# A gated attention and mlp block on one core: value products split by columns, the first attention turn beside the mlp's last tile, mlp in text order, statistics fetched apart

## The chip, the cores and the metric

The kernel runs on one core of a Trainium2 chip. The metric is the device time of one execution in microseconds (us). The core's engines are named as in the profile: PE is TensorE (matmul), PEld its weight load, DVE VectorE, ACT ScalarE, POOL GpSimd, SP SyncE, which here only issues DMAs. Each engine works through its own queue of instructions in order and waits on semaphores for the others.

## What is computed

The input is x of 2048 tokens by 448. Cut to what matters, the reference is:

```python
g = sigmoid((x * gate_w).sum(-1, keepdims=True))
# attention: 16 heads of 28 channels
q, k, v = split(x @ wqkv)
p = softmax(q @ k.T * 28 ** -0.5)
a = (p @ v) @ wo
# mlp: 448 -> 1792 -> 448
b = gelu(layernorm(x) @ w1 + b1) @ w2 + b2
return g * a + (1 - g) * b
```

Inputs and output are fp32. For most matmuls the kernel splits each fp32 factor into a high and a low part in float32r, and adds three products (high by high, high by low, low by high).

## The kernel before, in words

TensorE's order is written by hand over the whole kernel. For the other engines a scheduler sets the order from dependences in the first two stages, and the text's order holds in the attention (`manual_schedule` at L664). The PSUM accumulator is one tile of eight banks of 512 fp32 columns.

Stage 1, the projections (L219 to L260). For each of four chunks of 512 tokens, `qk_tile` makes 7 tiles of q and k (11 matmuls of 512 columns, L168) that go through ACT and DVE to DRAM, and `v_tile` makes 4 tiles of v. Between them lie the layernorm statistics: `ln_stats` loads two token tiles and runs bn_stats and bn_aggr on DVE (L196 to L199), `ln_rows` makes the columns of mean and 1/deviation, and `ln_turn` (L207 to L214) turns them into rows: for each of the two a transpose on PE, a copy on DVE, a DMA to `lns`. `ln_turn` runs twice, for 4 and for 12 token tiles, and both of its loop's steps use one bank. `ln_load` reads the rows back, spread over all partitions; `ln_apply` normalises a tile of x on POOL and ACT.

Stage 2, the mlp (L472 to L498). For each chunk of 512 tokens, `mlp1(f)` makes 14 tiles of the hidden layer (11 matmuls each into bank f % 2), with the gelu twice on ACT (L454, L455) and the low part `hl` on POOL (L456). `mlp2(c, i)` then makes four output tiles of 42 matmuls (L463, L464, L466), copied on ACT to `h` (L469) and stored to `gbs` (L470). In chunk 0 the weights are loaded as they are needed: `load_w1` splits on ACT and POOL (L93, L94), `load_w2` on ACT and DVE (L99, L100). All share a staging buffer `r` of three (L85).

Between the mlp's matmuls lies other work for PE. A softmax needs the largest score of each query first; the class `RowMax` makes those maxima with single score products (L321) of 512 keys, reduced on DVE, one bank (L301) or two (L303) at a time. The class `Filler` hands them out: in the mlp in groups of six products into banks 2 to 7, spread evenly over its slots (476 of 1040 of them there), and in the attention up to three per turn, evenly (`due`).

Stage 3, the attention (L664 to L715). A unit is one score tile of 128 keys by 512 queries of one head; four units, one per head of a group of four, make a step. A turn does five units: three, then two, each with three products (L629), in banks 0 to 4, and an exp over three banks and one over two (L634), with up to three row maxima in banks 5, 6, 5. The third uses the bank of the first, and so waits for DVE's reduce of the first. Behind the scores, `pv_mm` (L655) adds the value products of the steps whose exps an earlier turn has made: four matmuls in fp32, one per head, in four column groups of 32 of the array, 512 columns each, into bank 7 (L658). 205 turns do 256 steps, so 153 turns add one step and 51 turns two. When 16 steps have been summed, `finish` normalises the result, in parts spread over later turns (`STEPS`); in the last group it goes on to the output projection.

At the seam between the mlp and the attention, the gate's exp and reciprocal (L611 to L614) come first; on SP's queue come the last store to `gbs` (L470), a load of b2 (L679), and the four loads of wo (`load_wo`, L590), each of which DVE casts to `woh` (L593) between the reduces of turns 1 to 4.

Of the kernel before, what the change touches and what calls it, by code (L numbers as in the profile page):

```python
# [7 lines left out]
F32 = mybir.dt.float32  # L8
# [7 lines left out]
P = 128  # L16
# [18 lines left out]
LQ = 12  # L35
STEPS = (2, 5, 7, 8, 9, 10)
# [3 lines left out]
def kernel(ctx: ExitStack, tc: tile.TileContext, xt, wqk, wv, wo, xk, w1, b1, w2, b2,  # L40
# [43 lines left out]
    def staged(width):  # L84
        return my.tile([P, CH], F32, name="r", bufs=3)[:, :width]  # L85

    def load_w1(f):
        r = staged(CH)
        nc.sync.dma_start(r, w1[f].rearrange("p t x -> p (t x)"))
        t = mw1.tile([P, 8, P], F32R, name=f"w1f{f}")  # L90
        w1h[f], w1l[f] = t[:, 0:4], t[:, 4:8]
        r = r.rearrange("p (t x) -> p t x", t=4)
# [3 lines left out]
    def load_w2(f):  # L96
        r = staged(D)
        nc.sync.dma_start(r, w2[f])
        nc.scalar.activation(w2h[f], r, AF.Copy)  # L99
        nc.vector.tensor_sub(w2l[f], r, w2h[f].bitcast(F32))  # L100
# [9 lines left out]
    def ln_fetch(c, t):  # L110
        lnx[c, t] = staged(CH)
        nc.sync.dma_start(lnx[c, t], xt[t, :, c * CH:(c + 1) * CH])
# [12 lines left out]
    with tc.tile_pool(name="qx", bufs=2) as qx, tc.tile_pool(name="qo", bufs=3) as qo, \  # L125
# [67 lines left out]

        def ln_stats(i):
            x = qx.tile([P, 2, D], F32, name="bxr")
            nc.sync.dma_start(x, xk[2 * i:2 * i + 2].rearrange("t p d -> p t d"))  # L196
            for n in range(2):
                nc.vector.bn_stats(st[:, 2 * i + n], x[:, n])
                nc.vector.bn_aggr(mv[:, 2 * i + n], st[:, 2 * i + n])  # L199
# [7 lines left out]
        def ln_turn(a, b):  # L207

            ps = next_ps()
            for n in range(2):  # L210
                r = qw.tile([b - a, P], F32, name=f"rows{a}{n}")
                nc.tensor.transpose(ps[:b - a, n * P:(n + 1) * P], mr[:, n, a:b], ident)
                nc.vector.tensor_copy(r, ps[:b - a, n * P:(n + 1) * P])
                nc.sync.dma_start(lns[n * NT + a:n * NT + b], r)  # L214
# [4 lines left out]
        for c in range(NC):  # L219
            for m in range(NM):  # L220
# [16 lines left out]
                if c == 0 and m in (3, 5):  # L237
                    ln_stats(m // 4)
                if c == 1 and m == 1:
                    ln_rows(0, TPC)  # L240
                if c == 1 and m == 5:
                    ln_turn(0, TPC)
                if c == 1 and m == 6:
                    ln_load(0)
                if c == 1 and m >= 4 or c == 2 and m < 3:
                    ln_stats(m - 2 if c == 1 else m + 5)
                if c == 2 and m in (0, 1, 2, 4):
                    ln_fetch(0, (0, 1, 2, 2, 3)[m])
                if c == 2 and 3 <= m < 6 or c == 3 and m == 0:
                    ln_apply(0, m - 3 if c == 2 else 3)  # L250
# [4 lines left out]
                if c == 3 and m < 3:  # L255
                    load_w1(m)
# [88 lines left out]
    class Filler:  # L345
# [11 lines left out]
        def spread(self, queue, upto, slots):  # L357
            if self.max is None:
                self.max = RowMax()
# [70 lines left out]


# [26 lines left out]
    def mlp2(c, i):  # L458

        sl = slice(i * P, (i + 1) * P)  # L460
        a = bank[:, i % 2, :D]
        for f in range(NF):
            nc.tensor.matmul(a, hh[f][:, sl], w2h[f], start=(f == 0), stop=False)  # L463
            nc.tensor.matmul(a, hh[f][:, sl], w2l[f], start=False, stop=False)  # L464
            filler.run(2)
            nc.tensor.matmul(a, hl[f][:, sl], w2h[f], start=False, stop=(f == NF - 1))  # L466
            filler.run(1)
# [4 lines left out]
    for c in range(NC):  # L472
        for f in range(NF):
            if c == 0 and f + 3 < NF:
                load_w1(f + 3)
            if c == 0 and f == 0:
                for k in range(4):
                    load_khr(0, k)
            if c == 0 and f == FS:
                filler.spread(nc.sync, MLP_MAX, (NC * NF - FS) * 23)  # L480
            if c == 0:
                load_w2(f)
            mlp1(f)
        if c == NC - 1:
            m0.close()
            aq = ctx.enter_context(tc.tile_pool(name="aq", bufs=1, side="right", reuse_waits="tile"))
            load_khi(0)
            load_klo(0)
            load_q(0)
            load_v(0)  # L490
            load_qm(0)
        else:
            ln_load(c + 1)
        for i in range(TPC):
            if c + 1 < NC:
                ln_fetch(c + 1, i)
                ln_apply(c + 1, i)
            mlp2(c, i)  # L498
# [7 lines left out]
    U, UA = 5, 3  # L506
# [103 lines left out]

    tc.keep_in_program_order(nc.scalar.activation(gate, zall, AF.Exp, scale=-1.0))  # L611
    nc.vector.tensor_scalar_add(gate, gate, 1.0)
    nc.vector.reciprocal(gate, gate)
    nc.vector.tensor_scalar(ngate, gate, -1.0, 1.0, op0=OP.mult, op1=OP.add)  # L614

    filler.spread(nc.gpsimd, NG * NC * 65, ((NG * NC - 2) * NT + LQ - 1) * 4 // U)

    probs = {}

    def scores(units, most):  # L620

        def product(u, i):
            n, k, j = u // 4 // NT, u // 4 % NT, u % 4
            g, (qh, ql) = n // NC, qs[n]
            a, b, r = ((khi[g], qh, DH + 1), (klo[g], qh, DH), (khi[g], ql, DH))[i]
            r = slice(32 * j, 32 * j + r)
            nc.tensor.matmul(bank[:, u % U], a[r, k * P:(k + 1) * P], b[r], start=(i == 0), stop=(i == 2))  # L629

        def exps(units):
            t = ap.tile([P, len(units), CH], F32, name=f"pt{len(units)}")
            b = units[0] % U
            nc.scalar.activation(t, bank[:, b:b + len(units)], AF.Exp, scale=SCALE)  # L634
            for i, u in enumerate(units):
                probs[u] = t[:, i]

        first, last = units[:UA], units[UA:]
        if most > 0:
            filler.max.issue(5, 1, [(first[0] + 3) % 4])  # L640
        for i in range(3):
            for u in first:
                product(u, i)
        exps(first)
        for i in range(3):
            for u in last:
                product(u, i)
            if i == 0 and most > 1:
                filler.max.issue(6, 1, [(first[0] + 1) % 4, (first[0] + 2) % 4])
        if last:  # L650
            exps(last)
        if most > 2:
            filler.max.issue(5, 1, [(first[0] + 1) % 4, (first[0] + 2) % 4])

    def pv_mm(step):  # L655
        n, k = divmod(step, NT)
        for j in range(4):
            nc.tensor.matmul(pv[32 * j:32 * j + 32, :], vg[n // NC][:, k, 32 * j:32 * j + 32], probs.pop(4 * step + j),  # L658
                             start=(k == 0), stop=(k == NT - 1), skip_group_check=True)

    pv = bank[:, 7]
    E = mybir.EngineType
    steps = NG * NC * NT
    with tc.manual_schedule(engines={E.SP, E.Pool, E.Activation, E.DVE}):  # L664
        fin = None
        summed = 0
        ready = 0
        at = -1
        since = 0
        for u in range(0, 4 * steps, U):  # L670
# [27 lines left out]
            scores(units, min(3, filler.due()))  # L698
            ended = False
            while summed < ready and not ended:  # L700
                pv_mm(summed)
                summed += 1
                ended = summed % NT == 0
            ready = (units[-1] + 1) // 4
            since += 1
            if ended:
                n = summed // NT - 1
# [4 lines left out]
        while summed < steps:  # L712
            pv_mm(summed)
            summed += 1
# [54 lines left out]
```

## Time and profile before

| | us |
|---|---|
| median of three runs | 1151.25 |
| lowest and highest of them | 1142.76, 1155.83 |
| the profiled execution | 1146.98 |
| its span, first to last instruction | 1145.2 |
| stage 1, from the first matmul | 6.7 to 126.7 |
| mlp | 126.7 to 486.4 |
| attention and tail | 486.4 to 1145.2 |

The mean granted clock of TensorE was 0.991. Lines of the page and of answers on the trace name a group of instructions by line of the kernel, engine, operation, and the tiles written and read, with partitions x elements and a count (x8). In the timeline the first number is the start in us, the second the duration, and a bracket at the end gives the idle time of the engine just before, with what ended it. In the windows view each row is a stretch of the span, with the busy time and instructions of each engine, the granted clock (PEclk, 1.00 is full), the share of the DMA engines and GB/s.

### The profile page before, as it was taken

Reading aid. Unit: us, or ns where it says so; the run is one execution under the profiler, and the core shown is the slowest. Engines: PE = TensorE matmul, PEld = TensorE weight load, DVE = VectorE, ACT = ScalarE, POOL = GpSimd, SP = SyncE. Lnnn points to the kernel's source line nnn. Section 1 sums busy time; section 2 is a strip of 40 time slices with the busy share of each in tenths; the row PEclk is TensorE's granted clock in tenths of the full one; section 3 lists DMA queues with packets and bytes.
Section 4 is the critical chain, followed back from the end, with each engine's and each line's share of the span. In section 5 each row is a group of like instructions: output and inputs, shape, how many; then the busy total and the mean of one; then the engine's idle time right before and its main releaser. Section 6 shows DMA issues by size and latency. Waiting matters only on the chain.

```text
span 1145.2 us, 19823 instructions
## 1 busy us (share of the span) xinstructions
PE 1116.6 (98%) x8136; PEld 678.4 (59%) x8136; DVE 731.6 (64%) x1033; ACT 635.9 (56%) x668; POOL 331.0 (29%) x355
## 2 busy tenths in 40 slices
PE   6999989999999999989999999999999999999998
PEld 4778867777767777744444444444444444454556
DVE  3433287888878888666676766676676667646103
ACT  5324551132033032067887878878787887848463
POOL 4043367146044032011123012311222123444250
PEclk9999999999999999989999999999999999999999
DMA  8878643002100014062101211111121003002201
GB/s 269 277 217 303 208 141 88 25 9 68 47 23 18 25 30 114 25 168 72 30 12 36 52 40 40 36 27 39 31 64 36 18 19 91 12 25 68 66 26 49
DMA packets 53519, 84.35 MB, mean 74 GB/s; under 512 B 8676, under 2 KB 28660, under 8 KB 52628
## 3 DMA queue, kind: packets, MB, share of 16 engines
q1 hardware_dynamic: 49236, 76.96, 22.5%
q0 software_dynamic: 4192, 6.12, 2.1%
q8 instruction: 64, 1.05, 0.4%
q14 instruction: 27, 0.22, 0.1%
HBM read 56.40 MB, written 26.49 MB: 72 GB/s over the span
## 4 chain that ended last, share of the span: by engine, by line
PE 89%; DMA 4%; POOL 3%; DVE 2%; issue 1%; ACT 1%; SPq 0%; POOLq 0%; ACTq 0%; DVEq 0%
PE bank L658 22%; PE bank L629 20%; PE bank L321 15%; PE bank L451 10%; PE bank L168 4%; PE bank L466 4%; PE bank L463 4%; PE bank L464 4%; PE bank L184 2%; PE bank L525 1%; DMA bxr<-in_xk 1%; PE bank L526 1%; PE bank L527 1%; DMA xraw<-in_xt 1%; POOL hl L456 1%
## 5 line engine op out<-in xcount | busy, mean ns | idle before, releaser
L634 ACT ACTIVATE pt<-bank 128x1536 f32<-128x1536 f32 (+1 forms) x410 | 484.6, 1234 | 155.9 <-PE bank L629 155.9
L301 DVE TENSOR_REDUCE mx<-bank 128x1 f32<-128x512 f32 x624 | 413.4, 687 | 174.9 <-PE bank L321 161.0
L658 PE MATMUL bank<-pt,vg 128*32 128x512 f32 x2048 | 263.7, 606 | 0.0
L303 DVE TENSOR_REDUCE mx<-bank 128x2 f32<-128x1024 f32 x200 | 235.4, 1219 | 41.1 <-PE bank L321 41.0
L321 PE MATMUL bank<-khi,qd 28*128 28x512 f32 x512 | 241.6, 479 | 0.3 <-DVE mx L301 0.2
L321 PEld LDWEIGHTS bank<-khi,qd 28*128 28x128 f32 x512 | 92.3, 181 | 148.3 <-DVE mx L301 107.0
L629 PE MATMUL bank<-qh,klo 28*128 28x512 f32 x1024 | 179.0, 395 | 0.0
L629 PE MATMUL bank<-qh,khi 29*128 29x512 f32 x768 | 161.8, 484 | 0.3 <-ACT h L469 0.3
L451 PE MATMUL bank<-y,w1f 128*128 128x512 f32 x616 | 153.2, 400 | 0.6 <-ACT h L455 0.6
L451 PEld LDWEIGHTS bank<-y,w1f 128*128 128x128 f32 x616 | 113.8, 190 | 36.1 <-issue 12.5
L629 PE MATMUL bank<-ql,khi 28*128 28x512 f32 x768 | 133.6, 393 | 0.0
L456 POOL TENSOR_TENSOR hl<-h,hh 128x512 fp32r<-128x512 f32 x56 | 72.5, 1295 | 172.0 <-ACT h L455 160.8
L658 PEld LDWEIGHTS bank<-pt,vg 128*32 128x32 f32 x2048 | 45.7, 108 | 84.6 <-issue 83.1
L629 PEld LDWEIGHTS bank<-qh,klo 28*128 28x128 f32 x1024 | 90.2, 186 | 4.2
L321 PE MATMUL bank<-khr,qd 28*128 28x512 f32 x512 | 80.7, 467 | 7.3 <-DVE mx L303 4.2
L541 POOL DMA_DIRECT2D lt<-ob x15 | 10.8, 723 | 265.7 <-DVE ob L540 265.7
L466 PE MATMUL bank<-w2h,hl 128*128 128x448 f32 x224 | 85.1, 380 | 1.9 <-POOL hl L456 1.9
L469 ACT ACTIVATE h<-bank 128x448 f32<-128x448 f32 x16 | 8.7, 543 | 140.4 <-PE bank L466 140.4
L629 PEld LDWEIGHTS bank<-qh,khi 29*128 29x128 f32 x768 | 63.3, 183 | 36.8 <-ACT pt L634 32.1
L463 PE MATMUL bank<-w2h,hh 128*128 128x448 f32 x224 | 84.7, 378 | 0.3 <-ACT hh L454 0.3
L454 ACT ACTIVATE hh<-bank,b1s 128x512 fp32r<-128x512 f32 x56 | 38.4, 685 | 81.9 <-PE bank L451 81.8
L464 PE MATMUL bank<-w2l,hh 128*128 128x448 f32 x224 | 82.3, 368 | 0.0
(100 smaller groups left out, 1237.0 us busy)
## 6 DMA issues: line engine op xcount, KB each, us to landing
qk<-hl SPq DMA_DIRECT2D x28, 512.0 KB
xraw<-in_xt SPq DMA_DIRECT2D x16, 256.0 KB
vs<-vt SPq DMA_DIRECT2D x16, 256.0 KB
r<-in_xt SPq DMA_DIRECT2D x16, 256.0 KB
rc<-rls POOLq DMA_DIRECT2D x60, 64.0 KB, 2.2
bxr<-in_xk SPq DMA_DIRECT2D x8, 448.0 KB
r<-in_w SPq DMA_DIRECT2D x14, 256.0 KB
gbs<-h SPq DMA_DIRECT2D x16, 224.0 KB
```

Of the source, the lines that this page charges most:

```text
L168: nc.tensor.matmul(ps, a, b, start=(i == 0), stop=(i == len(ops) - 1))
L301: nc.vector.reduce_max(self.mx[:, c0:c0 + 1], bank[:, b0], axis=AX)
L303: nc.vector.reduce_max(self.mx[:, c0:c1 + 1:c1 - c0], bank[:, b0:b1 + 1], axis=AX)
L321: nc.tensor.matmul(bank[:, b], self.qds[self.n][r, i * P:(i + 1) * P], khi[self.n // NC][r, k * 512:(k + 1) * 512], start=True, stop=True)
L451: nc.tensor.matmul(ps, a, b, start=(i == 0), stop=(i == len(ops) - 1))
L456: nc.gpsimd.tensor_sub(hl[f], h, hh[f].bitcast(F32))
L463: nc.tensor.matmul(a, hh[f][:, sl], w2h[f], start=(f == 0), stop=False)
L464: nc.tensor.matmul(a, hh[f][:, sl], w2l[f], start=False, stop=False)
L466: nc.tensor.matmul(a, hl[f][:, sl], w2h[f], start=False, stop=(f == NF - 1))
L629: nc.tensor.matmul(bank[:, u % U], a[r, k * P:(k + 1) * P], b[r], start=(i == 0), stop=(i == 2))
L634: nc.scalar.activation(t, bank[:, b:b + len(units)], AF.Exp, scale=SCALE)
L658: nc.tensor.matmul(pv[32 * j:32 * j + 32, :], vg[n // NC][:, k, 32 * j:32 * j + 32], probs.pop(4 * step + j), start=(k == 0), stop=(k == N ...
```

## The change

The change has four parts.

1. Value products. `pv_mm` counts columns in place of steps, and does pieces of a step that are multiples of 128 columns. A new function `share(turn)` says up to which column a turn may go: the 16 steps of a chunk are spread evenly over the turns of that chunk, with a lag of 0.6 turns, and never beyond what earlier turns' exps have made. Of 205 turns, 134 take 640 columns, 44 take 768, 16 take 256 (the first of a chunk), and the others 512 or 1024. In all there are 402 pieces of 128 to 512 columns.

```diff
-    def pv_mm(step):
-        n, k = divmod(step, NT)
-        for j in range(4):
-            nc.tensor.matmul(pv[32 * j:32 * j + 32, :], vg[n // NC][:, k, 32 * j:32 * j + 32], probs.pop(4 * step + j),
-                             start=(k == 0), stop=(k == NT - 1), skip_group_check=True)
+    def pv_mm(upto):
+
+        nonlocal summed
+        while summed < upto:
+            step, a = divmod(summed, CH)
+            b = min(CH, a + upto - summed)
+            n, k = divmod(step, NT)
+            for j in range(4):
+                nc.tensor.matmul(pv[32 * j:32 * j + 32, a:b], vg[n // NC][:, k, 32 * j:32 * j + 32],
+                                 probs[4 * step + j][:, a:b], start=(k == 0), stop=(k == NT - 1), skip_group_check=True)
+            summed += b - a
+
+    def share(turn):
+
+
+        ready = turn * U // 4
+        n = min(NG * NC - 1, summed // (NT * CH))
+        first, last = (-(-NT * 4 * i // U) for i in (n, n + 1))
+        part = (turn - first - LAG) / (last - first - LAG)
+        return min(ready, steps, (n + 1) * NT) * CH if part >= 1 else min(ready * CH, n * NT * CH + int(NT * CH * part) // P * P)
...
-            scores(units, min(3, filler.due()))
-            ended = False
-            while summed < ready and not ended:
-                pv_mm(summed)
-                summed += 1
-                ended = summed % NT == 0
-            ready = (units[-1] + 1) // 4
+            if u:
+                scores(units, min(3, filler.due()), lambda n: ap.tile([P, n, CH], F32, name=f"pt{n}"))
+            before = summed // (NT * CH)
+            pv_mm(share(u // U))
+            ended = summed // (NT * CH) > before
```

2. First turn. `scores` moves ahead of the mlp unchanged, but for its exp tiles, which the caller gives. The mlp's last tile (chunk 3, tile 3) accumulates in bank 7 and has no row-max filler; after its fifth f the scores and exps of units 0 to 4 are issued, without row maxima, into the second buffers of `klo` and `vg`. The gate's exp and reciprocal come before the last chunk's second layer.

```diff
     def mlp2(c, i):
 
         sl = slice(i * P, (i + 1) * P)
-        a = bank[:, i % 2, :D]
+        last = c * TPC + i == NT - 1
+        a = bank[:, 7 if last else i % 2, :D]
         for f in range(NF):
             nc.tensor.matmul(a, hh[f][:, sl], w2h[f], start=(f == 0), stop=False)
             nc.tensor.matmul(a, hh[f][:, sl], w2l[f], start=False, stop=False)
-            filler.run(2)
+            if not last:
+                filler.run(2)
             nc.tensor.matmul(a, hl[f][:, sl], w2h[f], start=False, stop=(f == NF - 1))
-            filler.run(1)
+            if not last:
+                filler.run(1)
+            elif f == NF // 3:
+                scores(list(range(U)), 0, early)
```

3. MLP. SP, POOL, ACT and DVE go in text order. The staging buffers are two of their own, and in chunk 0 also the two halves of `lnr`, taken in turn. Fetching and splitting are apart: chunk 0 fetches w1 three f ahead and w2 of this f, then does `mlp1(f)`, then splits w1 of f + 2 and w2 of f − 1. The four parts of `khr` are loaded one per f, and the normalised tiles of the next chunk come behind the output tiles.

```diff
+    with tc.manual_schedule(engines={E.SP, E.Pool, E.Activation, E.DVE}):
+        for c in range(NC):
+            for f in range(NF):
+                if c == 0:
+                    if f + 3 < NF:
+                        fetch_w1(f + 3)
+                    fetch_w2(f)
+                    if f == 0:
+                        filler.max = RowMax()
+                    if f < 4:
+                        load_khr(0, f)
+                    if f == FS:
+                        filler.spread(nc.sync, MLP_MAX, (NC * NF - FS) * 23 - 3 * NF)
+                mlp1(f)
+                if c == 0:
+                    if f + 2 < NF:
+                        split_w1(f + 2)
+                    if f > 0:
+                        split_w2(f - 1)
...
+            for i in range(TPC):
+                mlp2(c, i)
+                if c + 1 < NC and i < 3:
+                    ln_apply(c + 1, i)
+                    if i < 2:
+                        ln_fetch(c + 1, i + 2)
+                    else:
+                        ln_apply(c + 1, 3)
```

4. Statistics. The loads of the token tiles are issued apart from bn_stats and ahead of it, `ln_rows` and `ln_turn` come one or two q and k tiles later, and `ln_turn` does both transposes, then one copy, then two DMAs.

```diff
             for n in range(2):
-                r = qw.tile([b - a, P], F32, name=f"rows{a}{n}")
                 nc.tensor.transpose(ps[:b - a, n * P:(n + 1) * P], mr[:, n, a:b], ident)
-                nc.vector.tensor_copy(r, ps[:b - a, n * P:(n + 1) * P])
-                nc.sync.dma_start(lns[n * NT + a:n * NT + b], r)
+            r = qw.tile([b - a, 2, P], F32, name=f"rows{a}")
+            nc.vector.tensor_copy(r, ps[:b - a, :2 * P].rearrange("p (n i) -> p n i", n=2))
+            for n in range(2):
+                nc.sync.dma_start(lns[n * NT + a:n * NT + b], r[:, n])
```

More of the change, by code (lines that the diff above doesn't have):

```diff
@@ L35 @@
 LQ = 12
+LAG = 0.6
 STEPS = (2, 5, 7, 8, 9, 10)
@@ L470, in mlp2 @@
         nc.sync.dma_start(gbs[c * TPC + i], gb)
[L472 to L480, printed above, removed]
-            if c == 0:
[L482 to L498, printed above, removed]
+    E = mybir.EngineType
@@ L608, in gate_acc @@
             nc.gpsimd.tensor_scalar(a, a, ngate[:, tt:tt + 1], None, op0=OP.mult)
[L611 to L614, printed above, removed]
     filler.spread(nc.gpsimd, NG * NC * 65, ((NG * NC - 2) * NT + LQ - 1) * 4 // U)
[L618 to L653, printed above, removed]
```

132 lines of the change are left out of this document (98 added, 34 removed).

## Prediction

> **What bounds the kernel now.** I read the busy table and the chain that ended last first, then the groups, and then stretches of the span (the windows view), which separate the three stages.
>
> ```profile
> PE 1116.6 (98%) x8136; PEld 678.4 (59%) x8136; DVE 731.6 (64%) x1033; ACT 635.9 (56%) x668; POOL 331.0 (29%) x355
> ...
> PE 89%; DMA 4%; POOL 3%; DVE 2%; issue 1%; ACT 1%; SPq 0%; POOLq 0%; ACTq 0%; DVEq 0%
> ```
>
> ```profile
> 6.70:126.70 120.00, 112.96 (x489) 93.41 (x490) 44.88 (x99) 44.44 (x79) 32.96 (x26) 0.99 0.84 269
> 126.70:175.30 48.60, 43.81 (x197) 31.64 (x196) 32.21 (x35) 30.95 (x52) 31.68 (x25) 0.96 0.53 155
> 175.30:192.00 16.70, 14.48 (x70) 11.23 (x69) 12.52 (x11) 4.11 (x7) 14.99 (x13) 0.90 0.20 60
> 192.00:486.40 294.40, 294.29 (x1501) 221.62 (x1499) 242.50 (x253) 65.27 (x106) 86.51 (x70) 1.00 0.14 41
> 486.40:505.10 18.70, 15.44 (x110) 7.37 (x111) 10.35 (x20) 11.39 (x11) 4.13 (x4) 0.73 0.62 165
> 505.10:1056.90 551.80, 551.54 (x5177) 263.38 (x5176) 373.93 (x590) 433.04 (x366) 132.53 (x182) 1.00 0.16 42
> ```
>
> The columns behind the stretch are its length, then the busy time of PE, its weight load, DVE, ACT and POOL, the granted clock, the DMA share and GB/s. TensorE is the bound: in 192.0 to 486.4 (the mlp after its first chunk) and 505.1 to 1056.9 (attention) it is busy without a hole at clock 1.00. What can be won by removing waits therefore lies in the four other stretches, where the PE columns leave 120.00 − 112.96 + 48.60 − 43.81 + 16.70 − 14.48 + 18.70 − 15.44 = 17.3 us idle, and where the clock is below 1. In the two full stretches only fewer or shorter matmuls help, and the change makes none.
>
> The half clock stands in four short stretches:
>
> ```profile
> 58.60:61.90 3.30, 2.96 (x8) 2.41 (x9) 1.08 (x4) 0.00 (x0) 0.00 (x0) 0.50 0.67 243
> 161.00:164.30 3.30, 3.30 (x9) 2.51 (x9) 2.89 (x4) 2.44 (x5) 1.80 (x2) 0.50 0.51 141
> 188.30:191.60 3.30, 2.94 (x8) 2.63 (x9) 1.77 (x2) 1.06 (x2) 2.56 (x3) 0.50 0.17 60
> 492.10:502.20 10.10, 9.09 (x48) 3.76 (x50) 5.64 (x10) 4.30 (x4) 3.39 (x3) 0.50 0.60 165
> ```
>
> **Value products by columns.** Turns of the attention in the timeline (start, duration, engine, line):
>
> ```profile
> 705.07 0.50 PE L321 MATMUL bank<-khi,qd 28*128 28x512 f32 x1
> 705.61 2.10 DVE L301 TENSOR_REDUCE mx<-bank 128x1 f32<-128x512 f32 x3 [0.62 <-PE bank L321]
> 706.15 2.37 ACT L634 ACTIVATE pt<-bank 128x1536 f32<-128x1536 f32 x2 [0.34 <-PE bank L629]
> 706.78 1.92 PE L658 MATMUL bank<-pt,vg 128*32 128x512 f32 x16
> 708.63 0.50 PE L321 MATMUL bank<-khi,qd 28*128 28x512 f32 x1
> 709.72 2.37 ACT L634 ACTIVATE pt<-bank 128x1536 f32<-128x1536 f32 x2 [1.20 <-PE bank L629]
> 710.34 1.06 PE L658 MATMUL bank<-pt,vg 128*32 128x512 f32 x8
> 711.34 0.50 PE L321 MATMUL bank<-khi,qd 28*128 28x512 f32 x1
> ```
>
> A turn begins with its first row maximum (L321). The score part lasts 706.78 − 705.07 = 1.71 in one turn and 710.34 − 708.63 = 1.71 in the next. The value part lasts 1.85 where two steps are summed (x16) and 1.00 where one is (x8). So a second step costs 0.85 and 0.15 of the first is fixed. Each part starts where the last ended, and the next turn starts directly behind the value part: PE is the sum of both, in turns with one step (2.71) and with two (3.56). Four turns with five steps cost 4 × 1.71 + 4 × 0.15 + 5 × 0.85 = 11.7. Spread evenly, with 640 columns in each turn, they cost the same 11.7. That is the point of this part: evening out moves columns from long turns to short ones, and where PE is full in both it moves no time. ACT's idle time (0.34 in a short turn, 1.20 in a long one) becomes more even, but it is not on the path.
>
> What the split adds is pieces. The code's rule gives 402 pieces of 128 to 512 columns in place of 256 steps, thus 146 more, each with four matmuls of other column groups. Nearest rows: a second step joins the first with no hole (0.85 each for 512 columns), which would give nothing for a further piece; the fixed 0.15 of a value part, were it due for every piece, would give 146 × 0.15 = 22. The part's 0.15 is drain before the next scores and is paid once per turn as now, so I take a value near zero, 2 us, with 0 and 22 as ends. A gain is excluded, since no product falls away. The Trainium skill, TensorE: Matmul & The Clock Gate, section "Wait — 56ns, not 53.3ns?", puts a fixed 2.5 ns on each matmul; an estimate by that page is 146 × 8 × 2.5 ns = 2.9 us at most, which would make the sum 0.9 higher, and no run here shows it alone.
>
> **Statistics.** The first turning of the statistics in the timeline:
>
> ```profile
> 58.94 0.08 PEld L212 LDWEIGHTS bank<-ident,mr 128*4 128x4 f32 x1 [4.06 <-DVE rows L213]
> 58.94 0.37 PE L212 MATMUL bank<-ident,mr 128*4 128x128 f32 x1 [3.65 <-DVE rows L213]
> ...
> 57.35 1.15 DVE L198 BATCH_NORM_STATS2 st<-bxr 128x6 f32<-128x448 f32 x2 [0.98 <-DMA bxr<-in_xk]
> 58.42 0.30 DVE L199 BATCH_NORM_AGGREGATE mv<-st 128x2 f32<-128x6 f32 x2
> 58.64 0.25 DVE L213 COPY rows<-bank 4x128 f32<-4x128 f32 x1
> ...
>   DVE rows L213: 8.9, 4
> ```
>
> The second transpose (L212) waits for the copy of the first (L213), which stands on DVE behind bn_stats, which waits for a DMA: PE idles 3.65. Behind it come 3.3 us of half clock, 2.96 of it busy, and half of that is lost: 1.5. The last row (all four waits of L212, PE and its weight load) leaves 8.9 − 4.06 − 3.65 = 1.2 for the second turning, 0.6 of it on PE. After, both transposes stand together ahead of one copy, so that none waits for DVE: −5.8 (range −6.4 to −4, if the one copy were late for the bank). The fetch of the statistics only moves earlier on SP's queue, past loads that are not late; nothing.
>
> **MLP in text order.** Chunk 0:
>
> ```profile
> 130.87 0.68 ACT L455 ACTIVATE h<-bank,b1s 128x512 f32<-128x512 f32 x1
> ...
> 148.53 0.50 PE L321 MATMUL bank<-khr,qd 28*128 28x512 f32 x2 [2.39 <-DVE mx L303]
> ...
> 159.12 0.50 PE L321 MATMUL bank<-khr,qd 28*128 28x512 f32 x2 [1.78 <-DVE mx L303]
> ...
> 185.44 0.47 PE L463 MATMUL bank<-w2h,hh 128*128 128x448 f32 x1 [0.34 <-ACT hh L454]
> ...
> 187.35 1.26 POOL L456 TENSOR_TENSOR hl<-h,hh 128x512 fp32r<-128x512 f32 x1
> ...
> 188.66 0.74 PE L466 MATMUL bank<-w2h,hl 128*128 128x448 f32 x1 [1.89 <-POOL hl L456]
> ```
>
> In the first layer PE waits 2.39 and 1.78 for row-max reduces, and one of the waits is followed by 3.3 us at half clock (161.0), half of it lost, 1.6. The change fetches weights three ahead, but on POOL the weight's low part now stands behind hl of the same f (1.26 each), and on DVE each w2 split stands ahead of the reduces. The third matmul of f+2 needs that weight: two gelus (0.68 each) and two POOL operations (1.26 each) come to 3.9 behind the end of f, in which PE does f+1 (48.60 / 14 = 3.5 now, holes and row-max products included) and two matmuls, so it just holds or just fails. A bound below is that all of this closes (−5.8); above, that the two lags last as long as two of today's (+4.2). I take +0.3, nothing in effect. In the second layer POOL normalises the next tokens ahead of hl, and PE waits 0.34 + 1.89 and runs 3.3 us at half clock (188.3, busy 2.94), 1.5 lost: 3.7. After, ln_apply stands behind the tile; I leave 1.1 for the last w2 split, now behind the last gelu: −2.6 (−3.7 to 0). The rows put half clock right behind a hole of 1.9 us. The Trainium skill, TensorE: Matmul & The Clock Gate, Part 1, lets the clock fall only after an idle window of about 3.4 us; by that rule the 1.5 would not come back with the wait, and the sum would be 1.5 higher; the trace disagrees, with half clock behind 1.89 us.
>
> **First turn beside the mlp's last tile.** The seam now:
>
> ```profile
> 486.63 0.54 ACT L469 ACTIVATE h<-bank 128x448 f32<-128x448 f32 x1 [8.13 <-PE bank L466]
> 487.19 0.32 SPq L470 DMA_DIRECT2D gbs<-h  x1
> 488.05 0.44 SPq L592 DMA_DIRECT2D ob<-in_wo  x1
> 490.65 0.49 PE L321 MATMUL bank<-khr,qd 28*128 28x512 f32 x1 [2.00 <-DVE mx L301]
> 492.42 0.40 DVE L593 CAST woh<-ob 128x448 fp32r<-128x448 f32 x1 [1.83 <-DMA ob<-in_wo]
> 492.73 1.28 DVE L301 TENSOR_REDUCE mx<-bank 128x1 f32<-128x512 f32 x2
> 493.47 0.79 PE L321 MATMUL bank<-khr,qd 28*128 28x512 f32 x1 [1.01 <-DVE mx L301]
> ```
>
> The turn moved is 15 score products and two exps, without row maxima: 1.7 on PE, now inside the mlp tile (end at E' = 486.4 + 1.7). The two exps and the earlier gate work on ACT lie beside the tile. But a chain is left as it is: tile end, copy (L469), its store, a bias load, the wo load on SP, wo's cast on DVE, and only behind it the reduces of turn 1 that its third row maximum waits for. It ends at 493.47, 7.1 behind the tile's end. Today turns 0 and 1 fill it; after, turn 1 alone does, with some 1.5 of PE, and PE idles about 5.6. So turn 1 ends 7.1 behind E' as before behind E, and what moved into the tile comes on top: +1.7. Ends: −7.4 (the chain does not bind, the holes of 2.00 and 1.01 and most of the half clock, 10.1 us at 0.50, go) and +4 (the longer hole lengthens the half clock by one such 3.3 us). I take +1.7, since the rows show the chain itself. The last tile's row-max groups go to other tiles at the same price: nothing.
>
> **Sum.** −5.8 (statistics) + 0.3 and −2.6 (mlp) + 1.7 (seam) + 2 (pieces) = −4.4. The profiled execution took 1146.98 (span 1145.2), 4.3 under the median of the three runs, 1151.25. From it the sum gives 1142.6, from the median 1146.9; I forecast 1144, between them.
>
> **Rivals.** Slower: each further piece pays the fixed 0.15 of a value part, as if the four column groups had to drain at every change of columns. Then the term is 22 in place of 2, and 1146.98 − 6.4 + 22 = 1163. It speaks for this that pieces of 128 columns are short against their weight loads; against it that steps of 512 join at 0.85. It decides from (11.5 + 6.4) / 146 = 0.12 us a piece (slower by 1%), from 0.04 it takes all the gain.
>
> Faster: the even turns use slack of the short ones.
>
> ```profile
> ACT pt L634 <- PE bank L629: 155.9, 204, 4.0
> ```
>
> ACT waits for PE in all turns (155.9 in 204), as it would if PE were full; slack would need PE to wait, and the score part is 1.71 in both kinds of turn. If half of the added 128 columns (0.21 of 0.85) vanished, 205 × 0.21 / 2 = 22 would go: 1146.98 − 4.4 − 22 = 1121.
>
> The wo chain does not bind, since the loads of that stretch (DMA share 0.62) have come earlier: −7.4 in place of +1.7 gives 1133.5.
>
> The text order makes chunk 0 worse: +4.2, no gain in the second layer, seam +4: −5.8 + 4.2 + 4 + 2 = +4.4, 1151, which is no change.
>
> **How the numbers follow.** Chances: the forecast 0.53, pieces 0.15, slack 0.09, wo free 0.13, text order worse 0.10. A measurement here tells about 1% (11.5 us) from no change. Faster by more: slack 0.09, most of wo free 0.10, and 0.05 of the forecast with several low ends, 0.24. Slower by more: pieces 0.15, and 0.05 for high ends together, 0.20. Within: 0.56. The forecast's own range is 1136 to 1150; the range that takes in the half-used slack and most of the dear pieces is 1121 to 1161.
>
> **What would show it.** In the changed profile: no idle before the transposes near 59 us and clock 1.0 there; no wait for hl in the first second-layer tile; a hole of 5 to 6 us ahead of turn 1's third row maximum, behind wo's cast, and half clock after it; exps of 1536 elements evenly some 2.92 apart, with the value part at about 0.15 + 0.85 × 1.25 = 1.21 of 640 columns. A value part above 1.3 speaks for dear pieces, a score part under 1.6 for slack. The forecast is wrong if even turns differ from 2.92 by over 0.06 (12 us in 205), or if the seam has no hole.

## The result, and the profile after

The changed kernel takes 1162.61 us (median of four runs, 1161.75 to 1164.46), the kernel before 1149.2 (four runs beside it): a ratio of 1.0133, with an interval of 1.0104 to 1.0161. It is slower by 1.3%. That is 1.6 us above the wide range of the forecast (1121 to 1161) and 12.6 above its own (1136 to 1150); its sum had a gain of 4.4. The profiled execution took 1162.36, with a span of 1160.6, 15.4 longer than before.

The windows view cut at the same places of the two programs shows where the 15.4 us arose. The columns are as in the prediction. First the kernel before, cut at the starts of the mlp's stages, at the seam, and at the exps of turns 3, 187 and 191 of the attention (its first two stretches, 6.7 to 126.7 and 126.7 to 175.3, stand in the prediction):

```profile
175.30:223.00 47.70, 45.48 (x236) 35.77 (x235) 38.49 (x40) 5.20 (x9) 22.55 (x19) 0.96 0.19 53
223.00:444.20 221.20, 221.20 (x1118) 163.47 (x1117) 185.40 (x195) 61.28 (x99) 75.38 (x59) 1.00 0.14 38
444.20:486.40 42.20, 42.09 (x219) 33.61 (x217) 31.12 (x31) 2.90 (x5) 3.57 (x5) 1.00 0.16 48
486.40:502.50 16.10, 12.84 (x88) 6.32 (x88) 8.23 (x16) 9.06 (x10) 3.39 (x3) 0.68 0.58 161
502.50:1056.90 554.40, 554.14 (x5201) 264.43 (x5199) 376.05 (x593) 435.36 (x368) 133.27 (x182) 1.00 0.16 43
1056.90:1079.60 22.70, 22.12 (x155) 14.12 (x153) 4.08 (x8) 9.47 (x8) 7.93 (x7) 1.00 0.09 32
```

Then the changed kernel, cut at the same events:

```profile
6.50:122.90 116.40, 113.81 (x488) 93.87 (x489) 45.64 (x97) 42.63 (x77) 31.17 (x24) 0.99 0.84 273
122.90:171.80 48.90, 44.95 (x198) 30.07 (x198) 31.61 (x32) 30.23 (x52) 34.74 (x25) 1.00 0.44 139
171.80:219.50 47.70, 46.30 (x242) 35.26 (x241) 43.07 (x46) 6.02 (x11) 16.59 (x13) 1.00 0.19 53
219.50:443.40 223.90, 223.56 (x1123) 164.01 (x1122) 191.90 (x199) 61.22 (x99) 82.92 (x65) 1.00 0.12 35
443.40:491.40 48.00, 45.91 (x222) 36.32 (x221) 22.66 (x27) 6.77 (x9) 1.65 (x2) 0.93 0.31 79
491.40:507.60 16.20, 10.39 (x77) 5.51 (x77) 5.74 (x10) 5.33 (x6) 5.66 (x7) 0.69 0.62 166
507.60:1066.20 558.60, 554.96 (x6268) 321.78 (x6266) 375.65 (x593) 435.32 (x368) 133.54 (x182) 1.00 0.16 43
1066.20:1094.90 28.70, 26.71 (x189) 17.23 (x185) 5.96 (x11) 9.49 (x9) 7.77 (x7) 0.88 0.07 26
```

Row by row, the end of stage 1 moves from 126.7 to 122.9 (3.8 gained), and the mlp's first chunk stays as it was (48.6 to 48.9, 47.7 to 47.7). From there everything is lost: 2.7 in the middle of the mlp, 5.8 in the last chunk's second layer, 0.1 at the seam, 4.2 in 184 turns of the attention, and 6.0 in four turns at its end. Two of these rows carry a clock below 1 that the kernel before does not have, 0.93 and 0.88.

**The last chunk's second layer (48.0 for 42.2).** Its beginning in the changed kernel's timeline:

```profile
444.93 1.28 ACT L573 ACT_TABLE_LOAD   x1
...
446.22 0.21 ACT L573 ACTIVATE gate<-zall 128x16 f32<-128x16 f32 x1
...
446.47 0.17 DVE L574 TENSOR_SCALAR gate<-gate 128x16 f32<-128x16 f32 x1 [2.96 <-ACT gate L573]
...
447.05 6.87 DVE L329 TENSOR_REDUCE mx<-bank 128x2 f32<-128x1024 f32 x6
...
448.32 0.50 PE L347 MATMUL bank<-khr,qd 28*128 28x512 f32 x2 [0.84 <-DVE mx L329]
449.45 0.62 PE L347 MATMUL bank<-khr,qd 28*128 28x512 f32 x2 [0.63 <-DVE mx L329]
...
450.58 0.79 PE L347 MATMUL bank<-khr,qd 28*128 28x512 f32 x2 [0.51 <-DVE mx L329]
```

DVE stands idle for 2.96 us with the reduces of a row-max group queued behind the gate's three small operations. These wait for ACT, which must first do two gelus and load a table. When DVE is free again it has two groups to reduce (x6), the next group waits for its banks three times, and half clock follows.

**The seam (16.2 for 16.1)** went as forecast:

```profile
493.08 0.45 SPq L686 DMA_DIRECT2D ob<-in_wo  x1
...
497.93 0.39 DVE L687 CAST woh<-ob 128x448 fp32r<-128x448 f32 x1 [23.88 <-DMA ob<-in_wo]
...
498.97 0.79 PE L347 MATMUL bank<-khr,qd 28*128 28x512 f32 x1 [5.80 <-DVE mx L327]
```

The third row maximum of turn 1 waits 5.80 us behind wo's cast (5.6 was forecast), 7.6 behind the tile's end at 491.4 (7.1).

**Turns 187 to 191 (28.7 for 22.7).** Turn 188 in the changed kernel:

```profile
1070.71 0.50 PE L347 MATMUL bank<-khi,qd 28*128 28x512 f32 x1
1070.82 0.68 DVE L626 SCALAR_TENSOR_TENSOR klo<-bank,gate,klo 128x448 f32<-128x448 f32 x1 [3.15 <-PE bank L621]
...
1071.42 0.68 DVE L327 TENSOR_REDUCE mx<-bank 128x1 f32<-128x512 f32 x1
...
1072.15 0.50 PE L347 MATMUL bank<-khi,qd 28*128 28x512 f32 x1 [0.95 <-DVE mx L327]
...
1073.69 0.28 PE L313 MATMUL bank<-ident,mf 128*16 128x128 f32 x1 [1.04 <-DVE mf L363]
```

These are the last row maxima of the kernel. They stand one behind the other with no scores between them, behind an output projection whose gating (L626) is first on DVE. In the kernel before, the last maxima and their transpose come a turn earlier, ahead of that projection. Where the clock was half in the changed kernel:

```profile
29.90:33.20 3.30, 3.30 (x9) 2.57 (x9) 0.00 (x0) 0.32 (x1) 0.00 (x0) 0.50 0.87 215
449.70:456.50 6.80, 6.29 (x18) 4.92 (x17) 4.22 (x4) 0.00 (x0) 0.00 (x0) 0.50 0.79 190
497.50:507.70 10.20, 8.73 (x59) 4.55 (x60) 5.74 (x10) 2.51 (x3) 5.66 (x7) 0.50 0.65 175
1074.40:1081.10 6.70, 6.70 (x41) 3.91 (x37) 0.00 (x0) 2.37 (x2) 0.64 (x1) 0.50 0.01 2
```

The second begins among the holes shown for the last chunk's second layer, the fourth right behind those of turn 188. The holes sum to 1.98 and 1.99 us, and half of the 6.29 and 6.70 us of busy PE is lost beside them. The Trainium skill, TensorE: Matmul & The Clock Gate, section "What's actually happening", has the clock fall after an idle window of about 3.4 us that runs freely; here it fell behind holes of 2 us in all, the longest single one 1.04, so the measurement decides.

**Even turns.** Exps of the attention, by their starts on ACT:

```profile
798.18 2.37 ACT L472 ACTIVATE pt<-bank 128x1536 f32<-128x1536 f32 x2 [0.55 <-PE bank L467]
801.14 2.37 ACT L472 ACTIVATE pt<-bank 128x1536 f32<-128x1536 f32 x2 [0.59 <-PE bank L467]
804.03 2.37 ACT L472 ACTIVATE pt<-bank 128x1536 f32<-128x1536 f32 x2 [0.52 <-PE bank L467]
807.16 2.37 ACT L472 ACTIVATE pt<-bank 128x1536 f32<-128x1536 f32 x2 [0.77 <-PE bank L467]
809.75 2.37 ACT L472 ACTIVATE pt<-bank 128x1536 f32<-128x1536 f32 x2 [0.22 <-PE bank L467]
```

The two turns with 640 columns (from 798.18 and 801.14) are 2.96 and 2.89 long, about as worked out (2.92). The turn that begins at 807.16 has 256 columns, and by PE's rate (1.71 + 0.15 + 0.43) should last 2.29; it lasts 2.59, with ACT idle for 0.22 only.

That turn is the exception, though. Of the 14 turns with 256 columns in this stretch, the other 13 last 2.76 to 2.85, and there DVE sets the length. One of them, turn 117:

```profile
844.33 0.50 PE L347 MATMUL bank<-khi,qd 28*128 28x512 f32 x1
844.54 0.69 DVE L634 COPY ob<-bank 128x512 f32<-128x512 f32 x1 [0.80 <-PE bank L714]
...
845.15 1.96 DVE L327 TENSOR_REDUCE mx<-bank 128x1 f32<-128x512 f32 x3
...
847.16 0.50 PE L347 MATMUL bank<-khi,qd 28*128 28x512 f32 x1 [0.21 <-DVE mx L327]
```

A turn with 256 columns is the first of a chunk, so DVE has to copy the finished chunk out of its bank (L634) ahead of the three reduces, and the next turn's first row maximum waits for the last of them: 847.16 − 844.33 = 2.83. In the turn at 807.16 a transpose stands in the place of the third maximum, so DVE has one reduce fewer. The kernel before has the same copy in the same turns; where such a turn sums one step (512 columns), it lasts 2.97 to 2.99 there. So 256 columns fewer save 0.15 in such a turn, while the other turns pay 0.43 for them; 14 × 0.28 comes to 3.9 of the 4.2.

### The profile page after: what moved, and what is told of

It reads as the page before. It is cut to its first block, busy times and chain, and to the rows that moved or that the text cites. A ratio compares the mean times of both kernels' runs of the same rounds, so it can differ in the third digit from the quotient of the medians.

```text
span 1160.6 us, 22156 instructions
## 1 busy us (share of the span) xinstructions
PE 1128.3 (97%) x9304; PEld 741.7 (64%) x9304; DVE 733.4 (63%) x1031; ACT 634.2 (55%) x668; POOL 334.3 (29%) x355
## 4 chain that ended last, share of the span: by engine, by line
PE 86%; DVE 6%; issue 3%; DMA 2%; POOL 2%; ACT 1%; SPq 0%; DVEq 0%; POOLq 0%; ACTq 0%
PE bank L714 21%; PE bank L467 19%; PE bank L347 13%; PE bank L513 10%; PE bank L180 6%; PE bank L530 4%; PE bank L526 4%; PE bank L527 3%; PE bank L196 2%; DVE mx L329 2%; DVE mx L327 2%; PE bank L619 1%; PE bank L620 1%; PE bank L621 1%; POOL w1f L103 1%
## 5 line engine op out<-in xcount | busy, mean ns | idle before, releaser
L714 PE MATMUL bank<-pt,vg 128*32 128x256 f32 (+3 forms) x3196 | 263.6, 446 | 0.0
L347 PE MATMUL bank<-khi,qd 28*128 28x512 f32 x512 | 234.8, 462 | 4.4 <-DVE mx L327 4.4
L467 PE MATMUL bank<-qh,klo 28*128 28x512 f32 x1024 | 194.1, 396 | 0.0
L467 PE MATMUL bank<-qh,khi 29*128 29x512 f32 x768 | 173.4, 478 | 0.3 <-ACT pt L472 0.3
L714 PEld LDWEIGHTS bank<-pt,vg 128*32 128x32 f32 x3196 | 81.6, 109 | 107.6 <-issue 96.9
L467 PE MATMUL bank<-ql,khi 28*128 28x512 f32 x768 | 145.1, 394 | 0.0
L467 PEld LDWEIGHTS bank<-qh,klo 28*128 28x128 f32 x1024 | 102.3, 186 | 1.6
L347 PE MATMUL bank<-khr,qd 28*128 28x512 f32 x512 | 85.9, 472 | 10.2 <-DVE mx L327 6.0
L467 PEld LDWEIGHTS bank<-ql,khi 28*128 28x128 f32 x768 | 77.3, 187 | 9.1
```

The source lines that it names most:

```text
L347: nc.tensor.matmul(bank[:, b], self.qds[self.n][r, i * P:(i + 1) * P], khi[self.n // NC][r, k * 512:(k + 1) * 512], start=True, stop=True)
L714: nc.tensor.matmul(pv[32 * j:32 * j + 32, a:b], vg[n // NC][:, k, 32 * j:32 * j + 32], probs[4 * step + j][:, a:b], start=(k == 0), stop=( ...
```

## The experiments

Each was run against the kernel before in the same session, and ratios are to that; its own median was 1148.43, 1144.61 or 1147.43 by session, so gains are to be read from the ratios. Stretches come from each run's profile.

**1. The gate's operations behind the first tile.**

```diff
-                nc.vector.tensor_scalar_add(gate, gate, 1.0)
-                nc.vector.reciprocal(gate, gate)
-                nc.vector.tensor_scalar(ngate, gate, -1.0, 1.0, op0=OP.mult, op1=OP.add)
...
                 mlp2(c, i)
+                if c == NC - 1 and i == 0:
+                    nc.vector.tensor_scalar_add(gate, gate, 1.0)
+                    nc.vector.reciprocal(gate, gate)
+                    nc.vector.tensor_scalar(ngate, gate, -1.0, 1.0, op0=OP.mult, op1=OP.add)
```

> The changed kernel, with the three DVE operations on the gate issued behind the last chunk's first second-layer tile in place of ahead of it (its exp on ACT stays where it is). Theory: in text order these three stand on DVE ahead of the row-max reduces and wait there for ACT's gate exp, so that the next row-max group waits three times (0.84 + 0.63 + 0.51 us) and 6.8 us of half clock follow; the last chunk's second layer, 47.97 us now, falls to about 42.6 and the time by 5.4, to 1157. Rival: the group waits because row-max groups now come every 14.55 slots and DVE can't keep up; then the three waits and the half clock stay, and the time moves by less than 1.

Measured: 1158.01, ratio 1.0079 (1.0060 to 1.0098). The last chunk's second layer takes 42.7. The same place in its timeline:

```profile
443.46 6.97 DVE L329 TENSOR_REDUCE mx<-bank 128x2 f32<-128x1024 f32 x6 [0.97 <-PE bank L347]
...
445.21 0.21 ACT L573 ACTIVATE gate<-zall 128x16 f32<-128x16 f32 x1
446.40 1.10 PE L347 MATMUL bank<-khr,qd 28*128 28x512 f32 x6
```

The group at 446.40 no longer waits, and the half clock is gone. Three operations of 0.6 us in all had cost 5.3 in this pair of profiles. How much of it is half clock differs by execution: the layer takes 45.1 to 48.1 in the profiles of experiments 2, 4, 6, 7 and 8, which leave the operations where they were. The groups' closer order was not the cause.

**2. The spread over one turn fewer.**

```diff
-    filler.spread(nc.gpsimd, NG * NC * 65, ((NG * NC - 2) * NT + LQ - 1) * 4 // U)
+    filler.spread(nc.gpsimd, NG * NC * 65, ((NG * NC - 2) * NT + LQ - 1) * 4 // U - 1)
```

> The changed kernel, with the row maxima of the attention spread over one turn fewer. Theory: since the first turn carries no row maxima and the count of slots starts with the second, the last maxima slipped by one turn, into the turn with an output projection, where each waits for the one before by way of DVE (0.95 + 1.04 us) and 6.8 us of half clock follow; with one turn fewer they end a turn earlier, as in the kernel before, both holes and the half clock go, and the time falls by 5 to 6, to 1157. Rival: the half clock there comes from the projection turns themselves; then it stays and the time moves by under 2.

Measured: 1163.16, ratio 1.0124 (1.0101 to 1.0148), no gain. Turn 188 still holds the last maxima:

```profile
1074.52 0.49 PE L347 MATMUL bank<-khi,qd 28*128 28x512 f32 x1 [0.95 <-DVE mx L327]
1076.04 0.28 PE L313 MATMUL bank<-ident,mf 128*16 128x128 f32 x1 [1.04 <-DVE mf L363]
```

The miss was in the edit: 1040 − 476 = 564 maxima at three a turn fill 188 turns exactly, and the code allows no more than three. This kernel therefore says nothing on either theory; the next does.

**3. One turn's maxima moved into the mlp.**

```diff
-MLP_MAX = 476
+MLP_MAX = 479
```

with the spread of experiment 2.

> The changed kernel with three row maxima more in the mlp (479 in place of 476) and the attention's spread over 187 turns. The edit before this one could not move them: 564 maxima at no more than three a turn need 188 turns, whatever the spread. Theory: with 561 left they end one turn earlier, ahead of the turn with an output projection; the waits of 0.95 and 1.04 us near 1070 and the 6.8 us of half clock behind them go, and turns 187 to 191 take 22.7 us in place of 28.7; the time falls by 5 to 6, to 1157. Rival: that stretch is slow because of the projection turns themselves; it stays at over 27 us.

Measured: the stretch behaves as the theory said, the time does not.

```profile
1065.50:1088.60 23.10, 22.51 (x186) 15.04 (x182) 4.09 (x8) 9.48 (x9) 7.50 (x7) 1.00 0.09 32
```

Turns 187 to 191 take 23.1 in place of 28.7 at full clock: the slipped turn was the cause of that stretch's 6.0. But the kernel takes 1162.38, ratio 1.0153 (1.0124 to 1.0182). In the profiled execution chunk 0's first layer took 55.6 in place of 48.9, with four waits of 0.63 or 0.64 for reduces and 6.8 us of half clock. At the end POOL's last drain took 10.97 us where it takes 1.42 in the others, and 5.5 of this were waited for. In this kernel the gate's wait did not hit a group (42.6 for that layer), since the groups lie elsewhere.

**4. wo later.** It is fetched and cast in the second chunk of the attention, each cast two steps behind its load.

```diff
-                    if 2 <= k < 6:
-                        load_wo(k - 2)
...
+                if n == 1 and 10 <= k < 14:
+                    if k >= 12:
+                        cast_wo(k - 12)
+                    fetch_wo(k - 10)
+                if n == 1 and k >= 14:
+                    cast_wo(k - 12)
```

> The changed kernel, with the four loads of wo fetched and cast during the second chunk's last steps of the attention (steps 26 to 31), each cast two steps behind its load, and no longer in turns 1 to 4. Theory: the 5.80 us in which PE waits for the second turn's third row maximum are due to wo's cast on DVE, which waits for a load that SP issues only behind the mlp's last store; without it the third maximum comes about 1.3 us behind the first, the hole and most of the 10.2 us of half clock go, and the time falls by 8 to 10, to 1153. Rival: the seam is held by the loads of the next queries and keys on SP or by the reduces themselves; then PE still waits over 3 us there and the gain is under 3.

Measured: 1156.63, ratio 1.0073 (1.0047 to 1.0099), 6 to 7 gained of the 8 to 10 expected. The seam:

```profile
490.52 0.50 PE L347 MATMUL bank<-khr,qd 28*128 28x512 f32 x1 [0.25 <-DVE mx L327]
```

The third maximum of turn 1 no longer waits; all that is left of the 5.80 is 0.25 ahead of turn 2, the row shown. The half clock is gone, and turn 3 comes 5.6 behind turn 1 in place of 15.0: 9.5 gained at the place. A part was lost again where the casts now stand. The loads of wo share two buffers, so the last one was issued only at 553.75, when POOL had finished with an earlier one (552.57 + 1.15 = 553.72), and its cast was late.

```profile
552.57 1.15 POOL L693 TENSOR_TENSOR wol<-ob,woh 128x448 fp32r<-128x448 f32 x1 [1.70 <-DVE woh L692]
...
553.75 0.32 SPq L688 DMA_DIRECT2D ob<-in_wo  x1
...
557.84 0.39 DVE L692 CAST woh<-ob 128x448 fp32r<-128x448 f32 x1 [2.41 <-DMA ob<-in_wo]
```

PE then waited 1.71 for a reduce at 558.9, with 10.2 us of half clock behind. A moved load takes its wait with it; in experiments 10 to 12 the loads stand two steps earlier.

**5. The three edits 1, 2 and 4 together.**

> The three edits together: gate operations behind the tile, row maxima over one turn fewer, wo fetched and cast later. Theory: the three losses lie at different places and add up: 5.4 + 5.5 + 9 = 20, 1142.5. Rival: one hole closed opens the next (the seam's other loads, or DVE), and less than 12 is gained.

Measured: 1151.46, ratio 1.0030 (1.0016 to 1.0043). Of the 20 expected, 11 to 12 came. Edit 2 gave nothing, as alone (5.5 of what is missing); the other two gave nearly the sum that each had alone.

**6. Value products in whole steps again.**

```diff
-        return min(ready, steps, (n + 1) * NT) * CH if part >= 1 else min(ready * CH, n * NT * CH + int(NT * CH * part) // P * P)
+        return min(ready, steps, (n + 1) * NT) * CH
```

> The changed kernel with the value products in whole steps again (a turn sums every step that is ready, up to the end of a chunk, as in the kernel before); everything else as changed. Theory: pieces cost nothing by themselves, but the light turns at the start of each chunk (256 columns, 2.59 to 2.83 us where 1.71 + 0.57 would fill them) waste time that the other turns pay back; without the split, turns 3 to 187 take 554.5 us as before in place of 558.7: 4 less. Rival 1: the even turns gained time and something else costs the 4 us; then it takes longer than 558.7. Rival 2: each of the 146 further pieces pays 0.15; then it would be 22 less, which the steady turns already speak against.

**7. The split without light turns.**

```diff
-LAG = 0.6
+LAG = 0.0
```

> The changed kernel with a lag of 0 in place of 0.6 turns: the first turn of a chunk takes 512 columns in place of 256, and there are 353 pieces in place of 400. Theory of light turns: no turn lies under 512 columns, each of the 16 chunks saves 0.2 to 0.5 us, and turns 3 to 187 take 551 to 555 us in place of 558.7. Theory of dear pieces: 47 pieces fewer of 400 with 146 added give a third of the 4.2 us back, 557.3.

Measured: whole steps 1154.0, ratio 1.0085 (1.0061 to 1.0108); lag 0 1154.51, ratio 1.0087 (1.0064 to 1.0109). Turns 3 to 187, first in whole steps, then with lag 0, by the windows view of each:

```profile
507.30:1061.70 554.40, 554.04 (x5201) 264.82 (x5199) 376.03 (x593) 435.46 (x369) 133.46 (x182) 1.00 0.15 43
```

```profile
506.00:1059.90 553.90, 553.70 (x5963) 307.82 (x5960) 376.00 (x593) 435.40 (x368) 134.04 (x182) 1.00 0.15 43
```

Both are the 554.4 of the kernel before, against 558.6. With lag 0 there are in this stretch still 95 pieces more than steps, some 760 matmul records more on PE (5963 for 5201), and they cost nothing. So pieces are free, even turns bring nothing, and the light turns cost the 4.2. In both kernels turns 187 to 191 also took 26.6 in place of 28.7, with 3.4 in place of 6.8 us of half clock; what else the ratios show is outside these stretches.

**8. The split of w1 ahead of the tile.**

```diff
+                if c == 0 and f + 2 < NF:
+                    split_w1(f + 2)
                 mlp1(f)
                 if c == 0:
-                    if f + 2 < NF:
-                        split_w1(f + 2)
```

> The changed kernel with the split of w1 for f + 2 issued ahead of the first layer's tile f in place of behind it, so that it stands on ACT ahead of f's gelus and on POOL ahead of f's low part. Theory: in chunk 0 PE waits for POOL's low part of the weights (1.01, 0.94, 0.17, 0.43, 0.48 us and a slower pace between), because on POOL it stands behind the low part of the hidden tile; these waits go, and chunk 0's first layer, 48.8 us, falls to 43 to 45, the time by 4 to 5. Rival: the waits are due to the fetch landing late; then ACT's split ahead of the gelus delays these too, and the layer takes 48 us or more.

In the changed kernel PE waited in chunk 0's first layer for the weight's low part, as the forecast's lag had it (129.58 to 157.67):

```profile
129.58 5.74 PE L513 MATMUL bank<-y,w1f 128*128 128x512 f32 x22 [1.01 <-POOL w1f L103]
136.26 2.79 PE L513 MATMUL bank<-y,w1f 128*128 128x512 f32 x11 [0.94 <-POOL w1f L103]
```

With the split ahead, none of these waits is left, but others have come:

```profile
141.82 0.50 PE L347 MATMUL bank<-khr,qd 28*128 28x512 f32 x2 [0.96 <-DVE mx L329]
142.95 0.50 PE L347 MATMUL bank<-khr,qd 28*128 28x512 f32 x2 [0.63 <-DVE mx L329]
```

Measured: 1157.35, ratio 1.0111 (1.0082 to 1.0141); the layer took 48.5 in this profile, with 3.4 us of half clock behind the new waits, and 45.9 in experiment 11, which has the same edit and no half clock. The fetch was not late. The waits were POOL's, and their gain is mostly given to DVE's.

**9. The kernel before with both transposes ahead of one copy, 10. the same with wo later, 11. the changed kernel with the edits 1, 4, 7 and 8, and 12. the same with 479 maxima and the spread of experiment 2.** In 10 to 12 wo is fetched in steps 24 to 27.

> The kernel before, with only the turning of the statistics changed: both transposes, then one copy, then two DMAs; the loads of the statistics stay where they were. Theory: the second transpose waits for the first copy, which stands on DVE behind bn_stats; without that wait stage 1 loses 3.65 + 0.37 us of idle and the half clock near 58.5, and the mlp starts at 121 in place of 126.7; the time falls by 5 to 6. Rival: the matmuls behind need x tiles that come by the same DMA queue and are late too; then the hole moves by some us and less than 2 is gained.

> The kernel before, with the statistics as in b_turn and wo fetched and cast in the second chunk of the attention (steps 24 to 30). Theory: the seam's holes (2.00 and 1.01 us) and most of its 10.2 us of half clock go as they did in the changed kernel, and the sum of both edits is 5.5 + 7 = 12.5: 1135. Rival: without wo's cast the reduces of turn 1 wait for the gate's operations on DVE, and only the 1.01 goes: 1141.

> The changed kernel with four edits: gate operations behind the tile, wo in the second chunk's steps 24 to 30, a lag of 0, and the split of w1 ahead of the tile. Theory: the losses found add up, from 1162.4: 5 + 9 + 6 + 3 = 23, 1139. Rival: as with the first three together, about two thirds of the sum arrive, 1147.

> The same four edits and the row maxima of one turn moved into the mlp (479). Theory: turns 187 to 191 take 23 in place of 28 us, 5 less than best_n, 1134. Rival: as when that edit stood alone, the mlp's first layer and the end of the kernel (POOL's last drain of 11 us) take it back: no less than best_n.

Measured: the transposes alone 1142.92, ratio 0.9968 (0.9944 to 0.9992); with wo later 1140.88, ratio 0.9938 (0.9914 to 0.9962); the four edits 1140.63, ratio 0.9951 (0.9926 to 0.9977); with 479 maxima 1140.82, ratio 0.9940 (0.9915 to 0.9966). In 9 the mlp starts at 121.4 in place of 126.7, 5.3 earlier, and PE's half clock at 58.5 is gone; in that execution chunk 0's first layer took 51.8 in place of 48.6 and the seam drew 13.6 us of half clock in place of 10.2, so the whole shows less. In 10 the seam lost its 1.01 and kept its 2.00, which is the rival's case:

```profile
485.51 0.79 PE L322 MATMUL bank<-khr,qd 28*128 28x512 f32 x1 [2.00 <-DVE mx L302]
```

In 11 all of the seam's hole is gone, and turns 187 to 191 still take 27.9. In 12 they take 22.6, and POOL's last drain takes 10.97 us again: the two cancel. All four beat both kernels of this case, the last three by about the same: 0.5 to 0.6% under the one before and, by the ratios, 1.8 to 1.9% under the changed one. The two edits of a few lines on the kernel before (10) do as well as the changed kernel with all its repairs.

## Why the prediction was wrong

Step by step, as the prediction had them, by the two profiles.

- **Statistics, −5.8.** Measured −3.8 at the mlp's start; alone (experiment 9) −5.3. The step was right. The changed kernel's profiled execution has 3.4 us of half clock at 29.9, behind holes of 1.21 and 0.64 that the kernel before has too, without half clock there.
- **First layer of chunk 0, +0.3.** Measured +0.3, by the lag that was named: waits for POOL's low part took the place of those for reduces.
- **Second layer of chunk 0, −2.6.** Measured 0. The wait for hl and the half clock went, but the closer row-max groups put one more group there and two waits for reduces of 0.63.
- **Row-max groups of the last tile, "to other tiles at the same price: nothing".** This failed twice. In the trace the last second layer has 38 row-max products where it had 50, and each of the other three has 71 where it had 65; the middle of the mlp became 2.7 longer, part of which the last tile saves. And the sentence overlooked that the first turn of the attention carried three maxima which it no longer has. With 564 maxima and three a turn there is no slack, so the last three slipped by a turn, into the one place where nothing covers them: +6.0 (experiment 3 takes it away).
- **The gate, "the earlier gate work on ACT lie beside the tile".** This failed. It priced the moved step on ACT and left out its three operations on DVE, which in text order stand ahead of the reduces and wait for ACT: +5.3 (experiment 1).
- **The seam, +1.7.** The hole came as forecast, 5.80 for 5.6, behind wo's cast (experiment 4). Turn 3 follows the tile's end by 16.1 us before and 16.2 after, so the moved turn's 1.7 went into the mlp with no gain, as worked out. This was the step with the widest range, and the one that came out best.
- **Value products, +2.** Measured 4.2, and the forecast's reason for it was wrong. A value part of 640 columns is 1.21 long in all 123 such turns of the stretch, as forecast, and pieces cost nothing (experiment 7). The step that failed is the claim that even spreading keeps the sum. It does while PE is full, but the list of turns that stands ahead of the prediction had 16 of 256 columns, each the first of a chunk. There DVE's copy and three reduces set a length of some 2.83, above PE's 2.29; even without the third reduce ACT's two exps (2.37 and 0.22 idle) hold the turn at 2.59. The prediction's rows, from 705 to 711, lie inside a chunk and hold no such turn.

The rival "dear pieces" gave 1163, which is the time measured, but its reason is refuted: the place was right by accident of size. It asked for a value part over 1.3, and 1.21 stood in the profile. "Slack" is refuted by experiment 6, "wo free" by the 5.80, and "text order worse" holds only as far as the gate's order on DVE is such a case; of what it placed in chunk 0, the second layer's missing gain came, but the first layer's +4.2 did not (+0.3).

The two failed steps add 5.3 + 6.0, the light turns 2.2 above the forecast, chunk 0's second layer 2.6, statistics 2.0, and the rest of the mlp's middle some 1 to 2: together some 19 to 20, which is the distance from −4.4 to +15.4.

What stays open: why POOL's last drain takes 10.97 us in the two kernels with 479 maxima, and how much of experiments 6 and 7 beyond the 4.2 is half clock that falls differently by run.

## What to carry to other kernels

When a step moves under text order, list its instructions on every engine, and for each engine what is queued behind it; a small operation that waits for another engine costs what it holds up, not what it runs. When work is dealt out at a fixed rate (three maxima a turn), check whether the rate has slack before taking a slot away: here the deal was full, and the last hand fell where nothing covered it. Evening out a load pays only where an engine idles in the light turns, and it must not make new turns so light that another engine's floor shows.

## What the runs showed of the hardware

Holes well under 3.4 us were followed by half clock: three of 0.84, 0.63 and 0.51 us within 3.1 us (6.8 us of half clock), 0.95 and 1.04 within 2.5 us (6.7), one of 1.71 (10.2), always in steps of about 3.4 us. Others were not: the 2.39 at 148.5 in the kernel before drew none. The pair of 1.21 and 0.64 near 28 us was followed by it in some executions and not in others of kernels with the same code there. So a hole is to be priced at its length plus, as often as not, half of a half-clock stretch of 3.4 to 10.2 us; this is an estimate from these rows.

The fp32 value products could be cut into pieces of 128 columns without any loss that these profiles resolve: 95 pieces more in 554 us left that stretch at its length.
